# Which quarters of the attention scores share a DMA queue, in a fused attention and gated-MLP kernel

## Chip, cores and metric

The kernel runs on one core of a Trainium2 chip. The metric is the device time of one execution in microseconds (us). Before the change the median of three runs is 756.28 us (755.79 to 757.04).

The engines are TensorE (PE, matmuls; PEld is its weight load), VectorE (DVE), ScalarE (ACT), GpSimd (POOL) and the sync engine (SP). Each runs its own instructions in its own order; they meet at semaphores. SP issues most transfers, POOL and ACT a few; the transfers of all three queues are carried by the same 16 DMA engines.

## The reference

`x` is 2048 x 1024 in bf16. It is normalized by row; the result `xn` goes into two branches, and their product is added back:

```python
xn = _layernorm(x, axis=-1)
s = _A_ref(xn, A_wqkv, A_wo)              # sliding dilated attention: 32 heads of 32, 8 taps 2 apart
g = _silu(_B_ref(xn, B_w1, B_w3, B_w2))   # gated MLP, 1024 -> 3584 -> 1024
return x + s * g
```

The attention of branch A looks at eight positions for each query, `pos - 2*w` for `w` = 0 to 7:

```python
idx = pos[:, None] - off[None, :]
...
logits = jnp.einsum("bhsd,bhswd->bhsw", q, kg) * scale
logits = jnp.where(mask[None, None, :, :], logits, -1e9)
attn = _softmax(logits, axis=-1)
o = jnp.einsum("bhsw,bhswd->bhsd", attn, vg)
```

## The kernel before

**Tiling.** The 2048 rows are cut into four chunks of 512 (`CH`), and two chunks make a block (`BL`). TensorE's products are formed for a block at a time from sums and differences of operand blocks (seven products where eight would be plain), so that VectorE and ScalarE have much adding and copying to do around every group of matmuls. The stages of a block are: q, k and v (`qkv_pairs`), the up projections of the MLP in 14 steps (`up_step`), the down projection (`mlp_down`, its operands loaded seven row tiles at a time as `w2` from the input or `t2` from a scratch `t_dram`), and the output projection with the gate (`wo`). All matmuls are issued at line 334, all VectorE tensor-tensor operations at line 343 (`tt`), all ScalarE copies at line 348, all plain transfers at line 357 (`dma`).

**Attention.** It uses no TensorE. For a chunk `c`, `attention(c)` (line 637) does these steps, all but the transfers and one exp on VectorE:

- for each tap `w`, `qk` products and halving sums (`qa`, `qb`, `qc`) leave partial scores in `E`, whose 128 partitions hold four partial sums for each of the 32 heads. `E` is cut into four quarters of 128 queries each (`sq`);
- four transfers (line 669) carry quarter `sq` of `E` into partitions `32*sq` to `32*sq + 31` of a tile `L`, in which one partition holds the four partial sums of one head next to each other. Each moves 256 KB;
- three adds `z` (lines 675 to 677) need all four quarters of `L`; then come a maximum tree (`tr`), a difference (`zd`), the exp on ScalarE (line 690), a sum tree, a reciprocal and a product `pb`, which gives the probabilities;
- four transfers (line 699) read partitions `32*sq` to `32*sq + 31` of `pb` and write each row to four partitions of `E[:, sq]`, that is, over all 128. Each moves 256 KB;
- the products `pv` (line 710) with `vT` need all four quarters of `E`, and their sums (`pa`) leave the output in `qo`.

On the profile `att<-E` is the first group of transfers (scores into `L`), `E<-att` the second (probabilities back). Chunk 0's are issued at about 136 and 169 us, chunk 1's at 303 and 339, chunk 2's at 482 and 505, chunk 3's at 612 and 639.

**Queues.** Of the four quarters of each group, 0 and 2 are issued by POOL, 1 and 3 by SP.

**The order of the instructions.** The kernel doesn't issue its operations in the order of the code. Each goes into a `Plan` with a planned duration (`occ`), or for a transfer a number of bytes and the length of its runs. `limits` works back from TensorE's order to a latest time for each; `simulate` walks through the operations with these costs and picks, for each engine but TensorE, the ready one with the earliest limit. That order is what is emitted. A transfer's planned time is made of its bytes and runs:

```python
    LAG = {SP: 1.4, ACT: 1.4, POOL: 2.2}
    ...
    def work(o):
        return o.nbytes / o.run / 16 * (0.0085 + o.run / 26500.0)
```

So the planned cost of a transfer or of an instruction decides which instruction is put ahead of which on its own engine, though it changes nothing in what the instruction does. `dma` has `kb` as its seventh argument and the run length as its eighth. In a step of the up projection, `ua2` (line 815) and `uh` (line 820) add a bank of TensorE's results to a saved part; the bank is free for the next matmul group when they are done. `um` (line 828) multiplies the two branches of the MLP.

`ln_td` (line 469) brings the normalized rows of block 1 into `xT` by transposing transfers, issued on ACT's queue.

Of the kernel before, what the change touches and what calls it, by code (L numbers as in the profile page):

```python
# [14 lines left out]
PE, DVE, ACT, POOL, SP = range(5)  # L15
# [209 lines left out]
def kernel(  # L225
# [14 lines left out]
    Dh, W, DIL = 32, 8, 2  # L240
# [11 lines left out]
    NR = 4  # L252
# [29 lines left out]
    E = const.tile([P, NST, W, P], BF16, name="E")  # L282
# [71 lines left out]
    def dma(eng, name, o, a, rd, wr, kb, run=1024, late=0.0):  # L354
        e = {SP: nc.sync, POOL: nc.gpsimd, ACT: nc.scalar}[eng]
        occ = {SP: 0.45, POOL: 0.58, ACT: 0.55}[eng]
        plan.op(eng, name, lambda: e.dma_start(out=o(), in_=a()), rd, wr, occ, 0.0, nbytes=kb * 1024, late=late, run=run)
# [5 lines left out]
    def xt_cells(half, kh, st=None):  # L363
        return [("xT", half, (kh * KH + k) * 2 + q // 2, q % 2) for k in range(KH)
                for q in (range(4) if st is None else [st])]
# [4 lines left out]
    def xs_cells(i):  # L370
        return [("xs", i, k) for k in range(KH)]
# [30 lines left out]
    def xrow(xt, st):  # L402
        return xt.ap().rearrange("p (s d) -> p s d", s=NST)[:, st, :]
# [65 lines left out]
    def ln_td(c, st, xt):  # L469

        half = c % 2
        plan.op(ACT, f"td{c}_{st}", lambda: nc.scalar.dma_start_transpose(  # L472
            out=xT[:, half, :, st * P:(st + 1) * P], in_=xrow(xt, st)),
            [(xt, st)], xt_cells(half, 0, st) + xt_cells(half, 1, st), 0.55, 0.0, nbytes=256 * 1024, run=256)

    def qkv_load(t):
        wts = []
# [84 lines left out]
    def qkv_sums(wts, early=0.0, hold=()):  # L562

        S = [plan.slot("r8", f"S{i}") for i in range(2)]
        w = lambda kh, r: (lambda: wts[kh].ap().rearrange("p (c j) -> p c j", j=NJ)[:, :, r * 4:r * 4 + 4])
        sv = lambda q: (lambda: r8v(S[q // 2], FP16)[:, (q % 2) * 2048:(q % 2 + 1) * 2048].rearrange("p (c j) -> p c j", j=4))
        c = lambda q: [(S[q // 2], q % 2)]
        tt("qs0", add, sv(0), w(0, 1), w(1, 1), wts, c(0), 2048, True, -early)
        tt("qs1", sub, sv(1), sv(0), w(0, 0), c(0) + [wts[0]], c(1), 2048, True, -early)
        tt("qs3", sub, sv(3), w(1, 0), sv(1), c(1) + [wts[1]], c(3), 2048, True, -early)  # L570
        tt("qs2", sub, sv(2), w(0, 0), w(0, 1), [wts[0]] + list(hold), c(2), 2048, True, -early)
        return S
# [64 lines left out]
    def attention(c):  # L637
# [28 lines left out]
        L = plan.slot("att", f"L{c}", 2)  # L666
        Lv = lambda r: L.ap().rearrange("p (r w n) -> p r w n", r=NR, w=W)[:, r]
        for sq in range(4):
            dma((POOL, SP)[sq % 2], f"L{c}", lambda sq=sq: L.ap()[sq * 32:(sq + 1) * 32].rearrange("h (r n) -> h r n", r=NR),
                lambda sq=sq: E[:, sq].rearrange("p w n -> p (w n)"), [("E", w, sq) for w in range(W)], [(L, sq)], 256, 2048)  # L670
        zf = lambda s: s.ap().bitcast(FP32)
        z = plan.slot("att", f"z{c}")
        zv = lambda: zf(z).rearrange("p (w n) -> p w n", w=W)
# [21 lines left out]
        pb = plan.slot("att", f"pb{c}")  # L695
        pbv = lambda: pb.ap()[:, 0:1024].rearrange("p (w n) -> p w n", w=W)
        tt(f"pb{c}", mul, pbv, zv, lambda: zt(zs)[:, 0:1].to_broadcast([P, W, P]), [z, zs], [pb], 1024, False)
        for sq in range(4):
            dma((POOL, SP)[sq % 2], f"E{c}", lambda sq=sq: E[:, sq].rearrange("p w n -> p (w n)"),
                lambda sq=sq: pb.ap()[sq * 32:(sq + 1) * 32, 0:1024].unsqueeze(1).to_broadcast([32, NR, 1024]),  # L700
                [pb], [("E", w, sq) for w in range(W)], 256, 2048)
        for jh in range(2):
            js = slice(jh * 4, jh * 4 + 4)
            A = lambda js=js: qo[:, u, js, :]
# [175 lines left out]
    def mlp_down(b):  # L880
# [82 lines left out]
        for g in G:  # L963
            if b + 1 < NB:
                ln_td(2 * b + 2, g, xn[0])
            prod(pb[g], g, 1, 0, rhs, False, FP16)
            tt("dsa", add, lambda g=g: f32(sp5[g]), pb[g].ap, lambda g=g: f32(sp5[g]), [pb[g], sp5[g]], [sp5[g]], 512, False)
            gsilu(2 * b + 1, 1, g, lambda g=g: f32(sp5[g]), [sp5[g]], 0.54)
        rhs = rhs_load("t", t=T4)
        for g in G:  # L970
            if b + 1 < NB:
                ln_td(2 * b + 3, g, xn[1])
            prod(pb[g], g, 1, 1, rhs, False, BF16)
            gsilu(2 * b + 1, 0, g, pb[g].ap, [pb[g]], 0.48)
# [151 lines left out]
    for b in range(NB):  # L1126
        c0, c1 = 2 * b, 2 * b + 1
        wq = qkv_load(0)
        if b == 0:
            plan.shift = -2.0  # L1130
            for st in range(NST):
                x_load(1, st, x1)
            plan.shift = -1.0
            for st in range(NST):
                ln_dve(1, st, x1)
            plan.shift = 0.0
            wk = qkv_load(1)
            qkv_first("q", wq, rows=rows0)
            qkv_first("k", wk, lambda j: ln_tp(1, j, x1, (ACT, ACT)))
            xn_sums()  # L1140
            sq = qkv_sums(wq, 30.0, xs_cells(1))
            for i in range(FH):
                w2_load(i)
                w2_sums(i)
            qkv_pairs(b, "q", wq, sq, first=True)
        else:
            attention(c0 - 1)
            xn_sums(hold=True)
            sq = qkv_sums(wq)
            wk = []  # L1150

            def second():
                xn_sum4()
                wk.extend(qkv_load(1))

            qkv_pairs(b, "q", wq, sq, second)
# [20 lines left out]
        for fb in range(FB):  # L1177
            up_step(b, fb)
        attention(c0)
        mlp_down(b)  # L1180
        wots = wo_load()
        wo_sums(wots)
        wo(c0, wots)
    attention(3)
    wo(3, wots)
    flush()
# [31 lines left out]
```

## Time and profile before

| What | Value |
|---|---|
| median of three runs | 756.28 us |
| the profiled execution's own time | 756.09 us |
| its span, first to last instruction | 754.3 us |
| mean granted TensorE clock | 0.986 |
| TensorE / VectorE / ScalarE busy | 721.3 / 640.5 / 377.2 us |
| `att<-E` on SP and on POOL, median from issue to landing | 8.3 and 8.5 us |
| `E<-att` on SP and on POOL, median from issue to landing | 7.1 and 6.4 us |
| `r<-t_dram` on SP, 896 KB, median from issue to landing | 6.5 us |

How to read the lines: in a line of the waits stand who waited for whom, the total in us, the number of times and the longest. In a timeline line stand the start, the length, engine, source line and operation, the tiles written and read, and the number of instructions merged; in brackets the idle time before them and what ended it. A table of stretches gives for each stretch the busy time of the engines with their counts, and at the end the granted TensorE clock as a share of full speed, the busy share of the 16 DMA engines and the GB/s that they moved.

### The profile page before, as it was taken

The page shows a single profiled execution, that of the slowest core. Times are in us where ns is not written, and L with a number is a line of the kernel's source. Part 1 is how long each engine was busy: PE and PEld are TensorE (multiplying, and loading weights), DVE is VectorE, ACT ScalarE, POOL GpSimd, SP SyncE. Part 2 cuts the span into 40 slices and gives each one's busy share as a digit, 9 for nine tenths or more (in the row PEclk, how much of TensorE's full clock was granted, in tenths as well). Part 3 has the DMA queues.
Part 4 walks back from the last instruction along what each step waited for, and adds up shares of the span by engine and source line. Part 5 has one row for each costly group of instructions (what it writes and reads, how often), then busy time and mean ns, then how long its engine had stood idle before and what let it go on. Part 6 is the DMA issues. An engine that isn't in the chain of part 4 may idle for free.

```text
span 754.3 us, 9156 instructions
## 1 busy us (share of the span) xinstructions
PE 721.3 (96%) x3372; PEld 346.3 (46%) x3372; DVE 640.5 (85%) x860; ACT 377.2 (50%) x656; POOL 25.5 (3%) x54
## 2 busy tenths in 40 slices
PE   8999999989999999886999999999999997999997
PEld 5655544434444444432455554444444443444443
DVE  6998999597999999167999699688999958699627
ACT  7753546375646698132354544664554645211233
POOL 0011000000000000000000000000000000000000
PEclk9999999999999999998999999999999999999999
DMA  9779865967545653999346449998555374744512
GB/s 332 282 273 395 284 201 186 222 220 200 195 142 168 239 190 118 173 226 264 113 118 216 143 143 318 239 275 277 171 179 188 115 172 153 223 148 145 168 70 97
DMA packets 127053, 150.54 MB, mean 200 GB/s; under 512 B 12320, under 2 KB 103968, under 8 KB 122656
## 3 DMA queue, kind: packets, MB, share of 16 engines
q1 hardware_dynamic: 113248, 121.65, 51.6%
q0 software_dynamic: 5312, 26.22, 10.7%
q10 hardware_dynamic: 8448, 2.10, 2.4%
q8 instruction: 26, 0.43, 0.3%
q14 instruction: 19, 0.16, 0.1%
HBM read 106.95 MB, written 32.51 MB: 185 GB/s over the span
## 4 chain that ended last, share of the span: by engine, by line
PE 66%; DVE 17%; DMA 10%; ACTq 3%; issue 2%; ACT 1%; SPq 0%; DVEq 0%
PE mm L334 66%; DVE att L343 6%; DVE h_sb L343 4%; DVE r L343 4%; DMA att<-E 3%; ACTq L472 3%; DMA E<-att 2%; DVE k L343 2%; DMA r<-in_A_wqkv_dram 2%; DMA r<-t_dram 1%; DVE qo L343 1%; DMA t_dram<-h_sb 1%; DMA h_sb<-in_B_w_dram 1%; DMA r<-in_A_x_dram 1%; DVE E L343 0%
## 5 line engine op out<-in xcount | busy, mean ns | idle before, releaser
L334 PEld LDWEIGHTS <-r 128*128 128x128 f16 (+1 forms) x2288 | 241.1, 108 | 259.8 <-issue 19.5
L334 PE MATMUL mm<-xs,r 128*128 128x512 f16 x1280 | 299.6, 381 | 12.3 <-DVE h_sb L343 11.1
L334 PE MATMUL mm<-xT,r 128*128 128x512 bf16 (+1 forms) x1008 | 228.2, 371 | 0.0
L334 PE MATMUL mm<-r,h_sb 128*128 128x512 bf16 (+1 forms) x704 | 157.8, 385 | 11.6 <-DMA r<-t_dram 5.9
L343 DVE TENSOR_TENSOR att<-att 128x2048 bf16<-128x2048 bf16 (+4 forms) x132 | 123.8, 950 | 47.4 <-DMA att<-E 38.1
L348 ACT COPY k<-mm 128x512 f32<-128x512 f32 x192 | 110.5, 589 | 87.8 <-PE mm L334 65.9
L334 PEld LDWEIGHTS <-h_sb 128*128 128x128 f16 (+1 forms) x800 | 79.0, 99 | 109.6 <-issue 11.3
L348 ACT COPY mm<-mm 128x512 f32<-128x512 f32 x88 | 48.7, 570 | 66.9 <-PE mm L334 32.1
L343 DVE TENSOR_TENSOR att<-qo,kT 128x2048 bf16<-128x2048 bf16 x64 | 77.1, 1214 | 4.6 <-ACT kT L348 4.6
L351 ACT ACTIVATE k<-k 128x512 bf16<-128x512 f32 x56 | 34.6, 631 | 89.5 <-DVE k L343 89.3
L343 DVE TENSOR_TENSOR att<-E,vT 128x2048 bf16<-128x2048 bf16 x56 | 66.3, 1215 | 0.0
L343 DVE TENSOR_TENSOR h_sb<-mm,k 128x512 bf16<-128x512 f32 x96 | 62.0, 679 | 0.4 <-PE mm L334 0.2
L343 DVE TENSOR_TENSOR r<-r,r 128x1024 f16<-128x1024 bf16 (+4 forms) x66 | 52.1, 794 | 3.4 <-DMA r<-in_A_wqkv_dram 3.1
L343 DVE TENSOR_TENSOR k<-mm,k 128x512 f32<-128x512 f32 x72 | 47.2, 680 | 9.0 <-PE mm L334 7.7
L351 ACT ACTIVATE h_sb<-mm 128x512 bf16<-128x512 f32 x60 | 35.2, 599 | 17.0 <-PE mm L334 17.0
L343 DVE TENSOR_TENSOR h_sb<-h_sb,k 128x1024 bf16<-128x1024 bf16 x56 | 36.6, 682 | 4.2 <-ACT k L348 4.0
L343 DVE TENSOR_TENSOR qo<-qo,att 128x2048 bf16<-128x2048 bf16 x32 | 38.9, 1215 | 0.0
L348 ACT CAST k<-mm 128x512 bf16<-128x512 f32 x56 | 32.5, 589 | 10.9 <-PE mm L334 10.6
L343 DVE TENSOR_TENSOR h_sb<-h_sb 128x512 f16<-128x512 bf16 (+1 forms) x72 | 36.4, 561 | 0.1
L343 DVE TENSOR_TENSOR r<-r 128x1024 f16<-128x1024 bf16 (+1 forms) x34 | 25.6, 774 | 0.0
L343 DVE TENSOR_TENSOR qo<-E,vT 128x2048 bf16<-128x2048 bf16 x8 | 9.8, 1219 | 18.6 <-DMA E<-att 18.6
L334 PE MATMUL mm<-r,xT 128*128 128x512 f16 x112 | 24.5, 379 | 0.0
(74 smaller groups left out, 349.4 us busy)
## 6 DMA issues: line engine op xcount, KB each, us to landing
r<-in_B_w_dram SPq DMA_DIRECT2D x42, 512.0 KB, 4.3
s_dram<-r POOLq DMA_DIRECT2D x14, 1024.0 KB, 4.8
r<-t_dram SPq DMA_DIRECT2D x16, 896.0 KB, 6.5
r<-s_dram SPq DMA_DIRECT2D x14, 1024.0 KB, 5.5
r<-in_A_wqkv_dram SPq DMA_DIRECT2D x12, 1024.0 KB, 6.9
r<-in_B_w_dram SPq DMA_DIRECT2D x12, 896.0 KB, 6.5
h_sb<-in_B_w_dram SPq DMA_DIRECT2D x14, 512.0 KB, 10.3
t_dram<-h_sb POOLq DMA_DIRECT2D x14, 512.0 KB, 5.7
```

Of the source, the lines that this page charges most:

```text
L334: nc.tensor.matmul(cut(ps.ap()), lhsT=lhs[k](), rhs=cut(rhs[k]()), start=(first and k == 0), stop=(last and k == n - 1), skip_group_check= ...
L343: plan.op(DVE, name, lambda: fn(out=o(), in0=a(), in1=b()), rd, wr, occ, 0.08, late=late)
L348: plan.op(ACT, name, lambda: nc.scalar.copy(out=o(), in_=a()), rd, wr, occ, 0.11)
L351: plan.op(ACT, name, lambda: nc.scalar.activation(out=o(), in_=a(), func=ACTF.Silu), rd, wr, occ, 0.11, table="silu")
L472: plan.op(ACT, f"td{c}_{st}", lambda: nc.scalar.dma_start_transpose(out=xT[:, half, :, st * P:(st + 1) * P], in_=xrow(xt, st)), [(xt, st)] ...
```

## The change

The quarters are given to the queues in another way: 0 and 1 to POOL, 2 and 3 to SP, for both groups of transfers. The planned size of each quarter goes from 256 to 330 KB, and the planned duration of a transposing transfer's issue from 0.55 to 1.3 us; these two change nothing in what is moved, only the order that the planner makes.

```diff
@@ ln_td
-            [(xt, st)], xt_cells(half, 0, st) + xt_cells(half, 1, st), 0.55, 0.0, nbytes=256 * 1024, run=256)
+            [(xt, st)], xt_cells(half, 0, st) + xt_cells(half, 1, st), 1.3, 0.0, nbytes=256 * 1024, run=256)
@@ attention
         for sq in range(4):
-            dma((POOL, SP)[sq % 2], f"L{c}", lambda sq=sq: L.ap()[sq * 32:(sq + 1) * 32].rearrange("h (r n) -> h r n", r=NR),
-                lambda sq=sq: E[:, sq].rearrange("p w n -> p (w n)"), [("E", w, sq) for w in range(W)], [(L, sq)], 256, 2048)
+            dma((POOL, SP)[sq // 2], f"L{c}", lambda sq=sq: L.ap()[sq * 32:(sq + 1) * 32].rearrange("h (r n) -> h r n", r=NR),
+                lambda sq=sq: E[:, sq].rearrange("p w n -> p (w n)"), [("E", w, sq) for w in range(W)], [(L, sq)], 330, 2048)
...
         for sq in range(4):
-            dma((POOL, SP)[sq % 2], f"E{c}", lambda sq=sq: E[:, sq].rearrange("p w n -> p (w n)"),
+            dma((POOL, SP)[sq // 2], f"E{c}", lambda sq=sq: E[:, sq].rearrange("p w n -> p (w n)"),
                 lambda sq=sq: pb.ap()[sq * 32:(sq + 1) * 32, 0:1024].unsqueeze(1).to_broadcast([32, NR, 1024]),
-                [pb], [("E", w, sq) for w in range(W)], 256, 2048)
+                [pb], [("E", w, sq) for w in range(W)], 330, 2048)
```

In the built programs TensorE's and POOL's orders are the same before and after. SP's differs in one place: of the two loads of the last `t_dram` operand of block 0's down projection (line 969), which stood behind chunk 1's two `E<-att` transfers, the first now stands ahead of them. ScalarE's differs by a few exchanged neighbours. VectorE's differs around the waits for the two groups of transfers and by exchanged neighbours elsewhere. Around the waits (the adds `z` wait for the scores, `pv` for the probabilities):

| Place | Before | After |
|---|---|---|
| chunk 0, scores | z z z ua2 ua2 uh | z z ua2 z uh ua2 uh |
| chunk 2, scores | z z z um um | z z um z um |
| chunk 2, probabilities | ua2 ua2 pv uh uh | ua2 ua2 uh pv uh |
| chunk 3, scores | z z ua2 ua2 z uh uh | z ua2 z uh ua2 uh z |
| chunk 3, probabilities | uh pv um um pv | um um pv |

## The prediction

> **What bounds the kernel now.** I read the page first (busy time), then the waits by engine, then the timeline of TensorE for every gap, then the timelines of VectorE and of the sync engine around the gaps, and last the table of stretches, for the rate of the DMA engines.
>
> ```profile
> PE 721.3 (96%) x3372; PEld 346.3 (46%) x3372; DVE 640.5 (85%) x860; ACT 377.2 (50%) x656; POOL 25.5 (3%) x54
> ...
> PE mm L334 <- DVE h_sb L343: 11.1, 7, 4.5
> PE mm L334 <- ACT k L348: 6.8, 4, 3.1
> PE mm L334 <- DMA r<-t_dram: 5.9, 1, 5.9
> ...
> DVE att L343 <- DMA att<-E: 38.1, 4, 16.9
> DVE qo L343 <- DMA E<-att: 18.6, 4, 8.2
> ```
>
> TensorE sets the time, so an edit gains only where TensorE stands still: 754.3 - 721.3 = 33.0 us, of which 11.1 + 6.8 + 5.9 lie at waits inside the kernel. VectorE waits four times for the scores (38.1 us) and four times for the spread probabilities (18.6 us). Those waits cost nothing by themselves, but VectorE works in order, and what stands behind them frees TensorE's banks:
>
> ```profile
> 153.84 3.20 PE L334 MATMUL mm<-xs,r 128*128 128x512 f16 x8 [3.10 <-DVE h_sb L343]
> 350.19 6.06 PE L334 MATMUL mm<-r,h_sb 128*128 128x512 f16 x17 [5.92 <-DMA r<-t_dram]
> 514.75 1.89 PE L334 MATMUL mm<-xs,r 128*128 128x512 f16 x8 [1.31 <-DVE h_sb L343]
> 628.27 3.21 PE L334 MATMUL mm<-xs,r 128*128 128x512 f16 x8 [4.48 <-DVE h_sb L343]
> ...
> 622.80 2.48 DVE L343 TENSOR_TENSOR att<-att 128x1024 f32<-128x1024 bf16 x2 [8.02 <-DMA att<-E]
> 625.20 1.28 DVE L343 TENSOR_TENSOR k<-mm,k 128x512 f32<-128x512 f32 x2
> 626.40 1.21 DVE L343 TENSOR_TENSOR att<-att 128x1024 f32<-128x1024 f32 x1
> 627.53 1.28 DVE L343 TENSOR_TENSOR h_sb<-mm,k 128x512 bf16<-128x512 f32 x2
> ...
> 628.20:631.40 3.20, 3.13 (x9) 0.57 0.00 0
> 631.40:635.00 3.60, 3.60 (x19) 1.00 0.81 254
> ```
>
> In chunk 3 VectorE stands 8.02 us for the scores; then three score adds (1.2 us each) and two adds on `k` run before the add into `h_sb` (`uh`, line 820), and TensorE, idle for 4.48 us, starts when that ends. In the two stretches shown last (length, TensorE busy with its count, granted clock, DMA share, GB/s) it then gets a clock of 0.57: eight matmuls take 3.2 us where eight take 1.89 at 1.00. So a long stall costs about 1.35 us on top. The clock is down behind 3.10 too (0.59 from 153.84) and behind 5.92 (0.50 from 350.1), but not behind the 1.29 at 500.86 (1.00). Chunk 2's score wait costs 1.29 + 0.17 us of TensorE in the same way (gaps at 500.86 and 502.06).
>
> ```profile
> 338.57 1.27 SPq L357 DMA_DIRECT2D E<-att  x2
> 339.92 4.72 SPq L357 DMA_DIRECT2D r<-t_dram  x2
> ...
> 139.90:146.00 6.10, 6.10 (x30) 2.74 (x28) 1.38 (x2) 3.20 (x6) 0.00 (x0) 1.00 1.06 128
> 304.00:306.00 2.00, 2.00 (x11) 0.94 (x10) 0.00 (x0) 0.13 (x1) 0.79 (x2) 1.00 1.09 382
> 340.00:341.00 1.00, 1.00 (x6) 0.49 (x5) 1.00 (x3) 0.10 (x1) 0.00 (x0) 1.00 0.95 111
> 508.00:509.00 1.00, 1.00 (x7) 0.42 (x5) 0.83 (x2) 0.63 (x1) 0.00 (x0) 1.00 0.87 193
> ```
>
> The first two lines: on the sync queue the last down-projection operand (`t_dram`, two halves, line 969) stands behind chunk 1's two writes into `E`, which wait for VectorE until 338.57, though the matmul that last read the first half's buffer ended at 330.6. The others are stretches (last two columns: DMA share, GB/s): while scores move the DMA engines are held full (1.06) at 128 GB/s, while weights and x move (304 to 306) as full at 382. One quarter alone, which touches 32 partitions on one side, gets 111. So a score transfer is bound by its 32-partition side, not by the engines.
>
> **The change part by part.** Nothing is added or removed: 32 quarter transfers stay, 16 on each queue, each 256 KB, issued in 0.56 us (GpSimd) or 0.61 us (sync). Two things move: which quarters share a queue, and, by the higher planned costs (330 instead of 256 KB, 1.3 instead of 0.55 us for a transpose), the planned order. The built orders differ on VectorE, in a few neighbours on ScalarE and in one place on the sync queue; TensorE's and GpSimd's are the same. The sum is made against the profiled run's 756.09 us (span 754.3 + 1.8 around it), 0.19 under the median of 756.28.
>
> (1) *Sync queue, chunk 1.* The first `t_dram` half now stands ahead of the two `E` writes. It can go at 330.6; by the median of such loads on the page (6.5 us) it is there by about 337, before TensorE needs it at 344.27. The second half stays behind the writes and takes the first one's place: landed about 350.15 instead of 353.38. TensorE does seven matmuls (1.5 us), waits until 350.15, and goes on 353.42 - 350.2 = 3.2 us earlier. If the low clock comes as before it lasts some 2.1 us longer behind that point, 1.05 us lost: 2.15. If the shorter wait (4.4 us) leaves the clock up, 3.75. I take **-2.5**, nearer the low end, since a 4.48 wait did lose the clock. Behind the moved load on its queue stand the two `E` writes; they wait for VectorE until 338.57 anyway, eight us after its issue.
>
> (2) *VectorE's order behind the waits.* Chunk 0: the first `uh` comes after three score adds and one `ua2` instead of two, 0.6 us sooner; but VectorE is busy 11.0 of the 11.2 us from 153.84, so the pushed-back adds return it: 0. Chunk 2: one `uh` now stands ahead of the wait for the probabilities, so the 1.31 stall shrinks to what the second `uh` costs, about 0.4: 0.9 gross, 0.5 kept. Chunk 3: `uh` comes after two score adds and one `ua2`, 2 x 1.25 + 0.6 = 3.1 us after the landing instead of 4.7: 1.6 gross; the third add, so the exp, is later, 1.0 kept. Together **-1.5** (bounds -3.1 and 0). The other swaps are neighbours of 0.3 to 1.2 us in stretches where TensorE has no gap over 0.6 us: 0, with 1 either way if that cover is gone.
>
> (3) *When the scores land.* Before, each queue's first quarter lies in partitions 0 to 63 and its second in 64 to 127, so both queues press on one half, then on the other. Now GpSimd's are both in 0 to 63, the sync engine's both in 64 to 127. No stretch shows two halves side by side from the two queues throughout, so I bound it. Low: nothing gained. High: 1.05 MB at 130 GB/s takes 8.1 us, at 2 x 111 GB/s 4.7: 3.4 sooner. I take 0.8 each, a quarter of it, nearer the low row, since the sync queue's packets start about 1 us before GpSimd's, both tails run alone, and an engine holding a slow packet of one queue doesn't serve the other. Chunks 0, 2 and 3 hold TensorE by it, stalls 3.10, 1.46 and 4.48, none used up: **-2.4**. Chunk 1 is hidden: VectorE waits 16.9 us, but TensorE's gaps there (2.55 and 3.12) end on ScalarE, whose queue is held by issues of transposes; 0, at best those two, at worst +1. The spreading back of probabilities (E) already reached 193 GB/s; 0, bounds -0.5 and +1.5 for each.
>
> [...]
>
> (4) *Clock.* Chunk 3's stall falls to 4.48 - 1.0 - 0.8 = 2.7 us, under the shortest that lost the clock (3.10): **-1.4**. In chunk 0 VectorE, full there, takes the same gain back: 0.
>
> Sum: -2.5 - 1.5 - 2.4 - 1.4 = -7.8, so 748.3 for the profiled run and **748.5** against the median; own range 745 to 751.5.
>
> **Rivals.** *The queues serialize, nothing lands sooner*: terms 1 and 2 alone, 756.3 - 4.0 = 752.3. For: DMA share is at 1.06 already; against: it is so at 128 GB/s where 382 is possible. [...]
> *The halves run fully side by side*: scores land 3.4 sooner, capped by the stalls left: 2.5 (chunk 0), 1.5, 2.9 (chunk 3 after 1.6 of order); with 1, chunk 2's order 0.5, chunk 3's 1.6 and the clock 1.4: -12.9, 743.4.
> *Slower: each queue's second quarter meets its own first.* Before, it found the other half fresh: 193 GB/s in 508 to 509, against 111 for a lone quarter. A quarter (262 KB) takes 2.36 us at 111 and 1.36 at 193: 1.0 later, 2.0 when the two queues' second quarters don't overlap; middle 1.5. Five transfers hold TensorE (scores 0, 2, 3 and probabilities 0, 2): +7.5 - 4.0 = +3.5, **759.8**. It decides from 0.8 us a transfer. Against: two queues on two halves should at least not press on one.
> *The planner's order gives the gains back*, as VectorE is at 20.00 of 20 us from 180 to 200: 756.3.
>
> **How the numbers follow.** Forecast 0.50, serialized 0.20, side by side 0.12, slower 0.12, given back 0.06. A measurement of this kernel can tell 0.2%, 1.5 us, from no change. Faster: 0.50 + 0.12 + 0.18 of serialized = 0.80; same: 0.06 + 0.02 = 0.08; slower 0.12. Range 741.5 to 757.5: it holds the side-by-side case with 2 us below, and the serialized and given-back ones, and leaves out most of the slower case and the tails.
>
> **What would show it.** Right: the first `t_dram` half lands before 340, one gap near 345 ending at the second half; score waits of VectorE under 34 us in all; the gap at 628 under 3 us with clock 1.00 behind it; the one at 514 under 0.6. Wrong: score transfers landing 8 to 11 us after issue as before (serialized), E transfers over 9 us (slower), or new gaps of TensorE behind VectorE in 155 to 260.

## The result, and the profile after

The changed kernel takes 752.31 us (median of 11 runs, 749.37 to 755.25), against 756.28 for the kernel before (11 runs): a ratio of 0.9934, 95% interval 0.9909 to 0.9960, or 4.0 us less. The forecast was 748.5; the rival in which the queues serialize and no score lands sooner was priced at 752.3.

First the head of the page of the changed kernel, then its waits (who waited for whom, total us, times, longest).

```profile
span 753.5 us, 9154 instructions
...
PE 719.8 (96%) x3372; PEld 346.0 (46%) x3372; DVE 640.6 (85%) x860; ACT 376.9 (50%) x656; POOL 25.5 (3%) x54
```

```profile
PE mm L334 <- DVE h_sb L343: 9.1, 8, 2.5
PE mm L334 <- ACT k L348: 7.8, 5, 3.2
PE mm L334 <- DMA r<-t_dram: 6.5, 1, 6.5
...
DVE att L343 <- DMA att<-E: 37.6, 4, 16.8
DVE qo L343 <- DMA E<-att: 13.9, 4, 5.1
```

The wait for the scores is as long as it was (37.6 against 38.1), TensorE's wait for `t_dram` is longer (6.5 against 5.9), and what fell is TensorE's wait for VectorE (9.1 against 11.1, the longest 2.5 against 4.5) and VectorE's for the probabilities (13.9 against 18.6). This profiled execution was the slowest of the eleven (755.25), so it shows where the time went better than how much. The timeline of TensorE in the same profile (start, length, tiles, count, in brackets the idle time before and what ended it):

```profile
154.18 1.02 PE L334 MATMUL mm<-xs,r 128*128 128x512 f16 x4 [2.33 <-DVE h_sb L343]
...
162.67 1.89 PE L334 MATMUL mm<-xs,r 128*128 128x512 f16 x8 [1.09 <-ACT k L348]
...
182.42 1.02 PE L334 MATMUL mm<-xs,r 128*128 128x512 f16 x4 [1.46 <-DVE h_sb L343]
...
352.83 7.54 PE L334 MATMUL mm<-r,h_sb 128*128 128x512 f16 x21 [6.54 <-DMA r<-t_dram]
...
516.09 1.02 PE L334 MATMUL mm<-xs,r 128*128 128x512 f16 x4 [0.89 <-DVE h_sb L343]
...
626.74 1.02 PE L334 MATMUL mm<-xs,r 128*128 128x512 f16 x4 [2.47 <-DVE h_sb L343]
627.93 1.54 PE L334 MATMUL mm<-xs,r 128*128 128x512 f16 x4 [0.17 <-DVE h_sb L343]
629.27 3.10 PE L334 MATMUL mm<-xT,r 128*128 128x512 bf16 x8
```

Three stalls behind attention's transfers shrank: 3.10 to 2.33 (chunk 0), 1.31 to 0.89 (chunk 2, behind the probabilities), 4.48 to 2.47 (chunk 3). In chunk 0 two later gaps, 1.09 and 1.46, take the gain back. Chunk 2's is not the same in every execution: in a second one of the changed kernel it is 1.36. VectorE in chunk 3 shows that the order did it and not an earlier landing:

```profile
623.12 1.23 DVE L343 TENSOR_TENSOR att<-att 128x1024 f32<-128x1024 bf16 x1 [7.87 <-DMA att<-E]
624.26 0.68 DVE L343 TENSOR_TENSOR k<-mm,k 128x512 f32<-128x512 f32 x1
624.87 1.22 DVE L343 TENSOR_TENSOR att<-att 128x1024 f32<-128x1024 f32 x1
626.00 0.68 DVE L343 TENSOR_TENSOR h_sb<-mm,k 128x512 bf16<-128x512 f32 x1
```

VectorE waits 7.87 us, as before (8.02); but the add into `h_sb` now starts 2.9 us after the landing instead of 4.7. That scores move no faster is seen in the stretches in which they have the DMA engines to themselves, here for the changed kernel and then for the one before (the last three columns: granted clock, DMA share, GB/s):

```profile
142.00:144.00 2.00, 2.00 (x11) 0.94 (x10) 0.69 (x1) 1.31 (x3) 0.00 (x0) 1.00 1.01 123
144.00:146.00 2.00, 2.00 (x11) 0.90 (x10) 0.00 (x0) 1.17 (x2) 0.00 (x0) 1.00 1.01 126
...
355.00:358.00 3.00, 3.00 (x9) 1.04 (x8) 3.00 (x5) 1.23 (x2) 0.00 (x0) 0.50 0.37 138
...
630.00:631.00 1.00, 1.00 (x4) 0.32 (x3) 0.93 (x3) 0.98 (x2) 0.00 (x0) 0.50 0.88 270
```

```profile
142.00:144.00 2.00, 2.00 (x11) 0.93 (x10) 0.00 (x0) 1.25 (x3) 0.00 (x0) 1.00 1.05 126
144.00:146.00 2.00, 2.00 (x11) 0.88 (x9) 0.00 (x0) 0.52 (x1) 0.00 (x0) 1.00 1.00 127
...
355.00:358.00 3.00, 3.00 (x15) 1.36 (x14) 3.00 (x6) 1.11 (x2) 0.00 (x0) 1.00 0.69 253
```

With each queue on its own half of the partitions the engines are as full (1.01) and as slow (123 and 126 GB/s) as with both queues on the same half. The rows at 355 and 630 are for the clock, taken up below.

**Stage by stage.** TensorE's instructions stand in the same order in all these kernels, so the start of one matmul in two traces tells how far the one is ahead. The table has the change of that shift over each stage, in us, against the profile before; negative is gained. The first three profiles have the changed planned order (two executions of the changed kernel, and one of a kernel with the old queues). The last has the old order and the new queues, and shows how far a stage scatters without a change of order.

| Stage (time in the profile before) | Forecast | After | After, again | Costs only | Regrouping only |
|---|---|---|---|---|---|
| head, to 145 | 0 | +1.10 | +1.79 | +0.26 | -0.04 |
| chunk 0, 145 to 200 | -0.8 | +0.71 | +0.14 | +1.13 | -0.16 |
| 200 to 317 | 0 | 0.00 | +0.01 | +0.22 | -0.55 |
| chunk 1, 317 to 360 | -2.5 | -0.06 | -2.71 | +0.11 | -1.53 |
| 360 to 450 | 0 | -0.23 | -0.23 | -0.22 | +1.00 |
| chunk 2, 450 to 530 | -1.3 | -1.04 | -1.11 | -1.03 | +1.73 |
| chunk 3, 530 to 740 | -3.2 | -1.32 | -1.72 | -2.59 | -0.93 |

Without the head, which lies ahead of the first wait for scores, the three with the changed order average -3.3 us: +0.7 in chunk 0, -0.9 in chunk 1, -1.1 in chunk 2, -1.9 in chunk 3, and -0.1 between. That is most of the 4.0 of the medians. The last column moves by as much in single stages (+1.7 in chunk 2), so a single stage of a single profile proves little.

### The profile page after: what moved, and what is told of

It is laid out like the page before. It is cut to its first block, busy times and chain, and to the rows that moved or that the text cites. A ratio compares the mean times of both kernels' runs of the same rounds, so it can differ in the third digit from the quotient of the medians.

```text
span 753.5 us, 9154 instructions
## 1 busy us (share of the span) xinstructions
PE 719.8 (96%) x3372; PEld 346.0 (46%) x3372; DVE 640.6 (85%) x860; ACT 376.9 (50%) x656; POOL 25.5 (3%) x54
## 4 chain that ended last, share of the span: by engine, by line
PE 60%; DVE 22%; DMA 11%; ACTq 3%; issue 3%; ACT 1%; SPq 0%; DVEq 0%; POOLq 0%
PE mm L334 60%; DVE att L343 8%; DVE h_sb L343 5%; DVE r L343 5%; ACTq L472 3%; DMA att<-E 3%; DMA r<-in_A_wqkv_dram 3%; DMA E<-att 2%; DVE k L343 2%; DMA h_sb<-in_B_w_dram 2%; DMA r<-t_dram 2%; DVE qo L343 1%; DVE xs L343 1%; ACT k L348 1%; DVE E L343 0%
## 5 line engine op out<-in xcount | busy, mean ns | idle before, releaser
L334 PEld LDWEIGHTS <-r 128*128 128x128 f16 (+1 forms) x2288 | 241.2, 108 | 259.1 <-issue 18.6
L343 DVE TENSOR_TENSOR att<-att 128x2048 bf16<-128x2048 bf16 (+4 forms) x132 | 123.9, 951 | 45.5 <-DMA att<-E 37.6
L334 PE MATMUL mm<-h_sb 128*128 128x512 f16 x96 | 22.0, 379 | 0.0
```

Source lines behind the costliest of these rows:

```text
L334: nc.tensor.matmul(cut(ps.ap()), lhsT=lhs[k](), rhs=cut(rhs[k]()), start=(first and k == 0), stop=(last and k == n - 1), skip_group_check= ...
L343: plan.op(DVE, name, lambda: fn(out=o(), in0=a(), in1=b()), rd, wr, occ, 0.08, late=late)
```

## Experiments

### Which part of the change does it

The regrouping alone, the planned costs alone, and the changed kernel once more. Of the two planned costs, the 330 KB alone makes the changed order, instruction by instruction, and the 1.3 us for a transpose alone leaves the old one.

```diff
# regrouping only, both groups of transfers
-            dma((POOL, SP)[sq % 2], ...
+            dma((POOL, SP)[sq // 2], ...
# costs only: 256 -> 330 in both groups, 0.55 -> 1.3 in ln_td; queues stay (POOL, SP)[sq % 2]
```

> The quarters regrouped (0 and 1 on GpSimd, 2 and 3 on the sync engine), the planned costs left at 256 KB and 0.55 us; the order of every engine is then that of before. Theory A (the whole gain comes from the planned costs, the queues serialize): 756.3, within 1 us, score landings of chunk 0 at 11.2 us after issue as before. Theory B (the forecast's third term): scores land 0.8 us sooner in chunks 0, 2 and 3, 753.9. Theory C (the regrouping makes the probabilities land later, as 9.54 against 8.73 us in chunk 0 and 9.52 against 8.14 in chunk 1 of the two profiles suggest): 757.1 to 757.7.

> The planned costs of after (330 KB, 1.3 us), so its order on every engine, but quarters 0 and 2 on GpSimd and 1 and 3 on the sync engine as before. Theory A: 752.3, as after. Theory B: 754.7, 2.4 us above after. Theory C: 751, about 1 us below after, with the probabilities of chunks 0 and 1 landing 0.8 to 1.4 us sooner than in after.

> The changed kernel once more, for a second profile: 749 to 755. If the first profile was a slow one of it, the head (up to 30 us) is about 1 us shorter and the gaps of TensorE behind the probabilities of chunk 0 (1.46 us) and at the second t_dram half (6.54 us) are smaller.

| Kernel | Median us (runs) | Ratio to before, 95% interval |
|---|---|---|
| regrouping only | 757.33 (12) | 0.9985, 0.9957 to 1.0014 |
| costs only | 753.52 (12) | 0.9945, 0.9923 to 0.9968 |
| the change again | 752.41 (10) | 0.9924, 0.9901 to 0.9947 |

The kernel before took 757.31 there (29 runs). The planned costs alone reach 0.9945, whose interval lies over most of the whole change's: they make most of the gain. The regrouping makes no difference that can be told. Both comparisons lean its way, by some 1.1 us alone (0.9985) and 1.6 us on top of the costs (0.9924 against 0.9945), but the first interval takes in 1 and the other two overlap, so a gain of one or two us is neither shown nor excluded by the times. The landing times show none. From issue to landing (least, median, most) chunk 0's four score transfers take, before and with the regrouping only:

```profile
DMA to landing us min/median/max: 6.2/9.1/11.2
```

```profile
DMA to landing us min/median/max: 6.1/9.1/11.3
```

### What a faster score transfer would be worth

Here each quarter goes to a quarter of the columns of all 128 partitions of `L`, with the same bytes, queues and old costs. The kernel then leaves out bringing a head's four partial sums together, so its output is not the reference's.

```diff
-            dma((POOL, SP)[sq % 2], f"L{c}", lambda sq=sq: L.ap()[sq * 32:(sq + 1) * 32].rearrange("h (r n) -> h r n", r=NR),
+            dma((POOL, SP)[sq % 2], f"L{c}", lambda sq=sq: L.ap()[:, sq * 1024:(sq + 1) * 1024],
```

> The kernel before, but each score transfer writes its quarter of E into all 128 partitions of L, 2 KB each, not into 32 partitions of 8 KB: the four partial sums of a head are not brought together, so the output is not the reference's. If the 32-partition side binds the scores: the four quarters of chunks 0, 2 and 3 land within 6 us of issue (1.05 MB at 300 to 380 GB/s and 2 to 3 us of start and finish) instead of 8.8 to 11.2, and the time is 3 to 7 us lower. If something else of these transfers binds them: landings as before, 756.

One execution took 734.01 us. Chunk 0's last quarter lands after 7.0 us instead of 11.2, and of TensorE's gaps behind scores only 0.7 us in one wait is left; what remains is one wait of 7.4 us for `t_dram`. The gain, some 23 us, is far more than the 3 to 7 us that were expected, though chunk 0's landing missed the 6 us. Part of the rest is chunk 1, which the forecast took for hidden: its two gaps that end on ScalarE (2.55 and 3.12 us) are gone as well, and TensorE gains 7.5 us between 317 and 335 us. So the forecast's place was right: TensorE is held by the landing of the scores, and there are some 20 us to be had there. The regrouping doesn't reach them.

### Is it 32 partitions, or 32 neighbours?

A quarter keeps its 32 partitions, but every fourth of the 128 (`4*h + sq`) instead of neighbours. `pb` is read in the same way, and the mask that lies on quarter 0 is brought to its partitions by one small transfer at the start.

```diff
-            dma(..., lambda sq=sq: L.ap()[sq * 32:(sq + 1) * 32].rearrange("h (r n) -> h r n", r=NR),
+            dma(..., lambda sq=sq: L.ap().rearrange("(h s) (r n) -> s h r n", s=NST, r=NR)[sq],
...
-                lambda sq=sq: pb.ap()[sq * 32:(sq + 1) * 32, 0:1024].unsqueeze(1).to_broadcast([32, NR, 1024]),
+                lambda sq=sq: pb.ap()[:, 0:1024].rearrange("(h s) n -> s h n", s=NST)[sq].unsqueeze(1).to_broadcast([32, NR, 1024]),
```

It was run with everything else as before, with the whole change, and with the changed costs but the old queues.

> The kernel before with its queues and planned costs, but a quarter lies in every fourth partition of L and pb (partition 4h + sq), not in 32 neighbours (32 sq + h); each quarter still touches 32 partitions on that side. One small transfer at the start brings chunk 0's mask to every fourth partition. If what binds a quarter is that its 32 partitions are neighbours: scores land in 4 to 7 us as in wide_scores, the probabilities also 2 us or more sooner than 7 to 9, and the time is 728 to 736. If it is that only 32 partitions take part, neighbours or not: landings and time as before, 756.

> The same on the changed kernel, so with 0 and 1 on GpSimd and the higher planned costs. If neighbours bind: the waits that the planned order eased are gone, so that order and queues are worth nothing more: within 1.5 us of spread_before, the higher planned cost at most harming. If not: 752.

> The spread quarters (every fourth partition of L and pb) with the changed planned costs, but with the old alternation of the queues. It splits the 5.3 us between the spread kernel with old costs (734.5) and the one with the whole change (729.3). If the planned order makes it, as it made the change's own gain (4 of 4 us): 729.3, within 1.5. If with spread partitions the regrouping counts by itself, for then a queue's two quarters no longer meet each other in the same way: 734.5, within 1.5. A value between says that both have a share.

| Kernel | Median us (4 runs) | Ratio to before, 95% interval |
|---|---|---|
| spread, else as before | 734.54 | 0.9706, 0.9659 to 0.9753 |
| spread, whole change | 729.25 | 0.9632, 0.9594 to 0.9671 |
| spread, changed costs, old queues | 728.67 | 0.9613, 0.9550 to 0.9676 |

All three beat both kernels. The waits of the one with the whole change:

```profile
DVE att L343 <- DMA att<-E: 16.1, 4, 8.6
...
PE mm L334 <- DVE k L343: 2.5, 1, 2.5
...
DVE qo L343 <- DMA E<-att: 1.0, 1, 1.0
PE mm L334 <- DMA r<-t_dram: 0.9, 1, 0.9
...
PE mm L334 <- ACT k L348: 0.7, 1, 0.7
PE mm L334 <- DVE h_sb L343: 0.6, 1, 0.6
```

VectorE waits 16.1 us for the scores instead of 37.6, and the three waits of TensorE, 23.4 us in the changed kernel (9.1 + 7.8 + 6.5), are 2.2; one of 2.5 us, for an add on `k`, is new. The expectation that the change would be worth nothing any more beside the spread quarters (within 1.5 us) was missed: it was 5.3 us. The third kernel says which part it was: with the old queues the gain is the same (728.67 against 729.25), so again the planned order and not the regrouping. Its interval and that of the spread kernel with old costs still touch; the waits point the same way, for VectorE stands 7.0 us for the probabilities with the old costs, 1.0 and 0.8 with the new ones.

### Apart, or into both halves?

Every fourth partition changes two things at once: neighbours are taken apart, and each quarter reaches into both halves of the partitions. Every other partition of one half (quarter 0 in 0, 2, ... 62, quarter 1 in 1, 3, ... 63, the other two in 64 to 127) changes only the first.

```diff
-            dma(..., lambda sq=sq: L.ap().rearrange("(h s) (r n) -> s h r n", s=NST, r=NR)[sq],
+            dma(..., lambda sq=sq: L.ap().rearrange("(a h b) (r n) -> a b h r n", a=2, b=2, r=NR)[sq // 2, sq % 2],
# pb and the mask in the same way
```

> The whole change, with a quarter's 32 partitions at every other partition of one half (0, 2, ... 62; 1, 3, ... 63; 64, 66, ...; 65, 67, ...) in place of 32 neighbours (752.4) or every fourth of all 128 (729.3). It asks what the spread quarters gain by: that neighbours are taken apart, or that a quarter reaches into both halves. If taking neighbours apart is enough, transfers land about as soon as with every fourth, 6 to 7 us for the scores: 729 to 736. If it is the reach into both halves, nothing lands sooner than with neighbours, 8 to 11 us, TensorE's gaps stay: 752.4, within 1.5. [...]

It took 744.19 us (4 runs), ratio 0.9808, 0.9761 to 0.9855: between the two, so neither expectation held for the whole. The landings of chunk 0 show why. In each fence the first line is for the score transfers, the second for the probabilities; the changed kernel, then every other partition, then every fourth:

```profile
DMA to landing us min/median/max: 6.2/9.1/11.2
...
DMA to landing us min/median/max: 5.1/7.0/9.5
```

```profile
DMA to landing us min/median/max: 6.2/9.1/11.4
...
DMA to landing us min/median/max: 3.2/4.6/5.5
```

```profile
DMA to landing us min/median/max: 4.4/5.8/7.0
...
DMA to landing us min/median/max: 2.4/3.5/4.2
```

The scores, which are written into the 32 partitions, gain nothing from being taken apart within a half (11.4) and 4.2 us from both halves (7.0). The probabilities, which are read from the 32 partitions, gain most of it by being taken apart (9.5 to 5.5, and 4.2 with both halves). Chunks 2 and 3 agree: the last quarter of the scores lands after 8.5 and 9.7 us in the changed kernel, 9.4 and 9.8 with every other partition, 5.2 and 7.6 with every fourth; of the probabilities after 7.0 and 7.6, then 5.8 and 6.0, then 5.3 and 4.8. In chunk 1 the scores do land sooner with every other partition (9.6 against 15.6), but there the old places alone scatter from 12.8 to 17.6 among the kernels.

### Chunk 1: the sync queue and `t_dram`

Three kernels move what stands ahead of the last down-projection operand: the changed kernel with chunk 1's four writes into `E` all on POOL; the changed kernel with the old 256 KB for chunk 1 alone, which puts both `t_dram` halves behind those writes again, and also reorders VectorE between about 328 and 427 us; and the first of these with the spread quarters.

```diff
# all of chunk 1's writes on POOL (also with the spread quarters)
-            dma((POOL, SP)[sq // 2], f"E{c}", ...
+            dma(POOL if c == 1 else (POOL, SP)[sq // 2], f"E{c}", ...
# chunk 1 with its old planned cost, both groups
-                ..., 330, 2048)
+                ..., 256 if c == 1 else 330, 2048)
```

> The changed kernel, but chunk 1's four writes of probabilities into E all go through GpSimd's queue, so that on the sync queue neither half of the last t_dram operand stands behind them. Theory: term 1 of the forecast failed because the second half still waits for VectorE behind those writes and lands at 352, so TensorE's gap only moves by seven matmuls. Then both halves are issued by 333 here, the gap of 5 to 6.5 us is gone, and the time is 4 to 6 us under after: 746 to 748. Rival: the loads are bound by what the DMA engines carry there (transposes, probabilities), the gap stays over 3 us, and the time is within 2 us of after.

> The changed kernel, but the planned cost of chunk 1's quarters alone is again 256 KB, so that on the sync queue both t_dram halves stand behind chunk 1's writes as before, and VectorE's order around chunk 1 is nearly the old one. If moving one half ahead is worth what the forecast said (2.5 us): 754.8. If nothing: 752.3, and TensorE leaves the gap at the last t_dram operand no later, measured against where it stood at 320 us, than in after.

> The spread quarters with the whole change, and chunk 1's four writes into E all on GpSimd's queue, so that nothing stands ahead of the last down-projection operand on the sync queue. In the run with the spread quarters alone chunk 1's part of the gain came without it: TensorE's gap of 6.5 us is what the edit took away before (749.4 to 752.4 against 748.4, so 4 us). If a gap at that operand is left with the spread quarters, TensorE starts the down projection 1 to 4 us sooner: 725 to 728. If the spread quarters had already let the writes go in time, nothing is left to gain: 729.3, and up to 1 us worse for GpSimd's four writes in a row.

| Kernel | Median us (runs) | Ratio to before, 95% interval |
|---|---|---|
| chunk 1's writes on POOL | 748.43 (4) | 0.9879, 0.9833 to 0.9925 |
| old cost for chunk 1 | 755.70 (10) | 0.9966, 0.9941 to 0.9990 |
| spread, chunk 1's writes on POOL | 727.78 (4) | 0.9598, 0.9551 to 0.9646 |

The timelines of the sync queue in the changed kernel, and of the sync queue and TensorE with the writes on POOL:

```profile
330.94 0.36 SPq L357 DMA_DIRECT2D r<-t_dram  x1
339.99 1.26 SPq L357 DMA_DIRECT2D E<-att  x2
341.34 2.34 SPq L357 DMA_DIRECT2D r<-t_dram  x1
```

```profile
329.47 3.15 SPq L357 DMA_DIRECT2D r<-t_dram  x2
...
335.74 20.67 PE L334 MATMUL mm<-r,h_sb 128*128 128x512 f16 x95
```

With nothing ahead of them both halves are issued from 329.47 on, and TensorE runs 95 matmuls without a gap at full clock where the changed kernel stands for 6.54 us: 9.2 us gained in chunk 1, of which 2.1 are given back by 450 us and another 1.0 by 530; 748.43 in the end. The old cost for chunk 1 costs 2.4 to 3.2 us by the ratios (0.9966 against 0.9934 and 0.9924), which speaks for a gain from moving one half; but the intervals overlap, VectorE's order moved along with it, and its profile shows no loss in chunk 1 (-1.3 us against before). With the spread quarters the edit gains nothing that can be told (0.9598 against 0.9632): the probabilities are there by themselves, and only a 0.92 us wait for `t_dram` was left.

## Why the forecast was half right

The direction, the lines where the change acts and the place were right, the size was not: 7.8 us forecast, 4.0 measured. Of its signs of being right, the first `t_dram` half landed before 340 (339.71), with one gap behind it, and the gap at 628 fell under 3 us; but the clock there fell, VectorE's score waits stayed above 34 us (37.6), and the gap at 514 above 0.6 (0.89). By its own steps:

**Term 3, the scores landing 0.8 us sooner (-2.4): this is the step that failed.** No sooner landing can be told: 6.2/9.1/11.2 in chunk 0 before and after, 126 and 123 GB/s, 38.1 and 37.6 us of waiting. Chunk 2's last quarter lands after 8.8 us before and 8.5 after, chunk 3's after 10.2 and 9.7, but with the changed order and the old queues chunk 3's takes 8.3, so those differences are not the regrouping's. The time alone would not refute the term: 2.4 us are a ratio of 0.9968, inside the interval of the regrouping alone (0.9957 to 1.0014). The term rested on reading 111 GB/s, the rate of one lone quarter (of the probabilities, at 340 us), as the limit of one half, to which a second half would add its own. Two queues on two halves together move 123 to 126 GB/s, as two on one half did, so there is no such sum. The rival named this.

**Term 4, chunk 3's clock (-1.4): in some executions only.** The stall fell under 3 us as the forecast said (2.47), and the clock fell nevertheless: in the changed kernel's profile it is 0.50 from 629 to 631, and eight matmuls take 3.10 us (629.27). In the second execution and in the costs-only kernel, TensorE in the same place:

```profile
624.00 3.16 PE L334 MATMUL mm<-xs,r 128*128 128x512 f16 x8 [2.31 <-DVE h_sb L343]
```

```profile
625.71 1.02 PE L334 MATMUL mm<-xs,r 128*128 128x512 f16 x4 [1.45 <-DVE h_sb L343]
```

A stall of 2.31 us lost the clock, one of 1.45 kept it. The step "under the shortest that lost the clock (3.10)" took the lowest case seen for a limit; what decides instead is worked out in the last section.

**Term 1, the moved `t_dram` half (-2.5): the mechanism as described, the size open between 0 and 3.** The first half was issued at 330.94 (forecast 330.6), TensorE went on into it and stood until the second half came, which is the 6.54 us gap. From there it went on at half clock, and for longer than the 2.1 us that the forecast added: in 355 to 358 nine matmuls run at a clock of 0.50, where before fifteen ran at 1.00, and the clock is whole again only near 359. Counted from 317 us, TensorE was 2.4 us ahead at the matmul that stands at 354 us before, and the half clock then took 2.3 of it, which leaves -0.06. With the costs only it was 1.0 ahead and lost 1.1 (+0.11). In the second execution the stall was 3.46 and the clock back by 355: 3.7 ahead, 1.0 lost, -2.71.

**Term 2, VectorE's order (-1.5): right in chunk 3, not shown in chunk 2.** Chunk 0 was put at 0, since VectorE, busy for 11.0 of 11.2 us there, returns what is pushed back; it returned a little more than it had gained (+0.1 to +1.1; the gaps at 162.67 and 182.42 weren't there before, apart from 0.26 us at the second). Chunk 2 gave 1.0 to 1.1 in the table, where order and earlier landing together were to give 1.3. But the stall behind the probabilities that the order was to shrink from 1.31 to 0.4 is 0.89, 1.36 and 0.92 in those three profiles, and 1.88 with the old cost for chunk 1, which has the same order here and gives only 0.2. Chunk 3 gave 1.3 to 2.6 with whatever clock it kept: its stall is 1.45 to 2.47 us in all five profiles of the changed order with neighbouring partitions, and 4.48 and 3.19 in the two of the old order.

**The rivals.** *Serialize, 752.3*, was terms 1 and 2 alone, and that is what came, to within the scatter. That the sum is met so closely (752.31) is luck: stage by stage chunk 3 gave more than its share, chunk 1 less, and chunk 0 lost. *Slower*: its sign, probabilities landing after more than 9 us, is there in chunks 0 and 1 (9.5 in both, 8.7 and 8.1 before), but in chunk 0 they take 7.9 with the regrouping alone and 9.9 with the costs only, so the regrouping isn't shown to cause it; and VectorE waits less for them, since more work now stands ahead of that wait. *Given back*: true of chunk 0 alone.

What stays open: why the second `t_dram` half lands at 351.6, 352.8 and 354.0 us in three profiles of the same order, which with the clock makes chunk 1 differ by up to 2.8 us; whether the regrouping is worth one or two us after all; and why, in chunk 0, the writes into 32 partitions gained only by both halves (11.4 to 7.0 us) and the reads from 32 mostly by being taken apart (9.5 to 5.5).

## What to carry to other kernels

Here the score transfers filled the DMA engines (1.06) at 128 GB/s, a third of the 382 that weights and x reached (1.09), and sorting them among the queues brought no gain that could be told (ratio 0.9985, 95% interval 0.9957 to 1.0014): look at which partitions such a transfer touches first. Spreading 32 partitions over all 128 cost a changed access pattern and took 3 to 4% off the whole kernel (ratios 0.9706, 0.9632 and 0.9613). And a planner's cost is an edit to the order: build the parts of such a change one by one, since the part in its title may not be the one that acts.

## What the runs showed of the hardware

**Neighbours and halves.** In chunk 0, quarters of 256 KB between two places on the chip moved at 123 to 128 GB/s with the engines full (share 1.00 to 1.06) when 32 neighbouring partitions were written; two queues on two halves together were no faster (123 and 126 GB/s against 126 and 127). With every fourth partition, at the same bytes and queues, chunk 0's last score quarter landed after 7.0 us instead of 11.2. So quarters in 32 partitions spread over the 128 landed as soon as the transfers over all 128 (7.0 us both in chunk 0).

**The clock and short stalls.** Stalls of TensorE of 2.33, 2.48 and 2.37 us in chunk 0 (two executions of the changed kernel, and costs only) left the clock at 1.00. Others halved it: 2.47 in the same place of the kernel with every other partition, 2.31 in chunk 3, and 2.06 at 333.46 with the spread quarters and chunk 1's writes on POOL.

```profile
154.40 3.18 PE L334 MATMUL mm<-xs,r 128*128 128x512 f16 x8 [2.47 <-DMA r<-in_B_w_dram]
```

The longest that kept it is 3.22 us (the changed kernel in chunk 1, clock 1.00 in the two us behind it), so between 2.1 and 3.2 us both were seen, and the longer ones, of 3.26, 3.46, 3.68, 5.42 and 6.54 us, lost it.

The traces show what decides. In each of the thirteen, all changes of the granted clock lie on one grid with steps of 3.413 us, and half clock lasts one, two or three steps. Here are two pairs of neighbouring steps of the changed kernel, around the stalls of 2.33 and of 2.47 us (after the step come its length and TensorE's busy time; the granted clock is the third number from the end):

```profile
150.37:153.78 3.41, 1.48 (x7) 0.59 (x6) 3.38 (x5) 0.63 (x1) 0.00 (x0) 1.00 1.21 294
153.78:157.20 3.42, 2.85 (x13) 1.26 (x13) 3.42 (x7) 2.44 (x5) 0.00 (x0) 1.00 0.65 156
624.88:628.29 3.41, 1.38 (x6) 0.57 (x6) 3.41 (x6) 1.61 (x3) 0.00 (x0) 1.00 0.70 223
628.29:631.70 3.41, 3.41 (x10) 1.18 (x8) 3.27 (x6) 3.39 (x6) 0.00 (x0) 0.50 0.51 168
```

TensorE was busy for 1.48 us of the first step and the next kept full clock; it was busy for 1.38 of the third and the next ran at half. The same border holds throughout: of the steps at full clock from 20 us on, the 2676 that were followed by full clock were idle for at most 0.59 of their length, and the 29 that were followed by half clock for at least 0.59. So in these traces a stall counts by how it falls on the grid. As an estimate from these figures, one under 2.0 us (0.59 x 3.413) would not lose the clock by itself, and one over 4.0 (twice that) would not keep it, however it is split between steps; the border is shown for this kernel's traces alone.
